# Late expert slots of an attention + two-layer-mixture kernel: rectifier in two halves over separate PSUM banks, weight scale step at the start of the split, last store inside the last branch

## The chip, the core and the metric

The kernel runs on one core of a Trainium2 chip. The core has a matrix engine (TensorE, PE in the profile, with its weight loads as PEld), three engines for elementwise work (VectorE = DVE, ScalarE = ACT, GpSimd = POOL), SyncE (SP), which issues most DMAs here, and 16 DMA engines. Each engine has its own instruction queue, worked off in order; queues wait for each other through semaphores. Matmul results land in PSUM (8 banks of 128 x 512 f32), everything else lives in SBUF.

The metric is the device time of one execution in microseconds, as the median of several executions: 1108.17 us for the kernel before (3 runs, 1105.92 to 1108.96).

## The reference, cut to what matters

```python
x = attention(q, k, v)          # queries pooled in pairs: 4 x 576 rows of 8 heads x 64 -> x is 2304 x 512
x = rational(x @ w_in) @ w_out  # w_in 512 x 2048, w_out 2048 x 512
logits = x @ w_gate             # 2304 x 8
e_idx = np.argmax(logits, axis=1)
for e in range(8):              # every token goes to one expert
    mask = e_idx == e
    h = np.maximum(x[mask] @ w1[e], 0.0)                                  # 512 x 1024
    out[mask] = gate_w[mask, None] * eom[mask, e, None] * (h @ w2[e])     # 1024 x 512
```

Only the last loop, the experts, is touched. How many tokens each expert has is known only while the kernel runs.

## The kernel before, in words

**Precision.** Every f32 operand of a matmul is kept as two f16 parts, high and low, and a product is three matmuls: high x high, high x low, low x high. A scale (a power of two) brings each operand into the range of f16; it comes from the largest absolute value.

**Stages.** Attention, the rational layer and the sorting of tokens by expert are recorded by a planner, which sets the order of every engine by a table and by costs; that part, with the first five blocks of experts' work, is not touched: its instructions stand in the same order before and after. The tokens, sorted by expert, lie in DRAM (`ysort`) and are worked off in slots of 128 tokens of one expert. Slots 0 to 4 (`NEARLY = 5`) are planned beside the last of the rational layer. Slots 5 and up, the late slots, are plain code: the functions `slot`, `from_slot`, `weights` and `changed` write instructions in the order in which they are called, and each engine works off its share in that order.

**A slot.** `slot_prep` loads 128 rows, finds their scale, splits them into high and low f16 and transposes them by DMA (`xTq`). `slot_g1` is the first product: 8 groups `fc` of 12 matmuls (L1476 to L1478), each group into 128 columns of one PSUM tile of 1024 columns (`sab0` or `sab1`, two banks each); then ACT writes the high part of the rectified result (L1483), DVE the low part (L1484), and DVE a scale (L1485). `slot_g2` is the second product: one DVE scale (L1504), 8 x 3 matmuls of 512 columns (L1494 to L1496) into `shared` or `hbs[0]`, ACT's scaled copy to SBUF (L1506), and POOL's indirect DMA to the tokens' places in the output (L1500, "the store").

**Order in the late slots.** `slot(s)` runs g1(s) and, around it, g2(s-1): from slot 6 to slot 16 the second product of the slot before stands behind the first product of this one, so PE has work while ACT and DVE rectify. In slot 17 (`NFULL - 1`) it also stands behind; from slot 18 (`NFULL`) on it stands ahead of g1(s), and the last slot's g2 comes alone at the end (`from_slot`, in the `Else`). Slot 18 and later ones sit in nested `If`s on the number of slots in use, which a register holds.

**Changing experts.** `changed(s, engines, fn)` reads a flag from SBUF into a register on each of those engines and branches: if slot s begins a new expert, its weights are split. `wsplit` gives the steps for one of the two weight matrices: DVE's largest value (4096 columns, L478), POOL's reduction over partitions (L1443), DVE's scale from it (`scale2`, L1422 to L1424), then four times ACT's high part (L500) and DVE's low part (L511) of 1024 columns, then DVE's copy of the inverse scale (L1450). `weights(s, xs, parts)` takes the steps in two parts: part 0 two slots ahead (the `SIZE` engines, DVE and POOL), part 1 one slot ahead or in the slot (the `SPLIT` engines, DVE and ACT). Of the 19 slots that this input uses, slot 18 alone begins a new expert among the late ones.

**The check.** Behind slot 9 `checks()` tests on the fly that the fixed scales fitted; it has one tiny matmul (L1008) into the bank `yps`.

**The end.** After the last store all engines read a number (L1801) and branch (L1802) on whether the first expert had too few tokens for the planned slots; that is not so here, and the branch jumps over the spare path, which holds a second, general copy of the whole kernel. Then the program's closing barrier (L1864).

Of the kernel before, what the change touches and what calls it, by code (L numbers as in the profile page):

```python
# [12 lines left out]
I32 = mybir.dt.int32  # L13
AF = mybir.ActivationFunctionType
# [329 lines left out]
def whole(tc, general, keep, checked, q, k, v, w_in, w_out, moe_a, moe_b, w_gate, w_ogate, w1, w2, out):  # L344
    nc = tc.nc
    V, S, G, T, SP = Steps(nc.vector), nc.scalar, nc.gpsimd, nc.tensor, nc.sync
    B, H, L, D = q.shape
    NT, DM = out.shape
# [8 lines left out]
    MUL, ADD, SUB, MAX = ALU.mult, ALU.add, ALU.subtract, ALU.max  # L357
# [4 lines left out]
    NEARLY = 5  # L362
# [15 lines left out]
    sab = [keep("psum", [128, 1024], F32, name=f"sab{i}") for i in range(2)]  # L378
    shared = keep("psum", [128, 512], F32, name="shared")
    sc_ = shared[:, 384:512]  # L380
    pvb = shared[:, 0:4 * (D + 1)].rearrange("p (n d) -> p n d", n=4)
    hbs = [keep("psum", [128, 512], F32, name=f"hps{i}") for i in range(2)]
    yps = keep("psum", [128, 512], F32, name="yps")
# [4 lines left out]
    def tiny(n, dt=F32):  # L388

        o = used[0]  # L390
        used[0] += n
        assert used[0] <= 944
        return small[:, o:o + n] if dt is F32 else small[:, o:o + n].bitcast(dt)
# [955 lines left out]
    FE = F // 128  # L1349
# [19 lines left out]
    rws = [zcut(RW, F32) for _ in range(5)]  # L1369
# [4 lines left out]
    obs = [zcut(DM, F32) for _ in range(2)]  # L1374
# [5 lines left out]
    xsm = [tiny(6) for _ in range(8)]  # L1380
    fst = tiny(4 * NE)
    fsti = tiny(4, I32)
    firstm = tiny(NE)
    padrows = keep("dram", [128, RW], F32, name="padrows")

# [48 lines left out]
    def wsplit(s, x, early=False):  # L1434

        fr = (raws1, raws2)[x][s % 3]
        m, M, sc, inv = (t[:, 2 * (s % 3) + x:2 * (s % 3) + x + 1] for t in (wm, wM, wq, wpn))
        fh, fl = ((w1h, w1l), (w2h, w2l))[x]
        steps = [({"DVE": 4.4}, amax(m, fr, AX.X))]
        if early:  # L1440
            steps += [m, lambda M: lambda e: scale2(M, m.bitcast(I32), sc, inv, 8)]
        else:
            steps += [({"POOL": 0.4}, lambda e: G.partition_all_reduce(M, m, channels=128,  # L1443
                                                                       reduce_op=bass_isa.ReduceOp.max)),
                      ({"DVE": 0.7}, lambda e: scale2(M, m.bitcast(I32), sc, inv))]
        for c in range(0, 4096, 1024):
            cs = slice(c, c + 1024)
            steps.append(({"ACT": 0.99, "DVE": 0.62}, hi(fh[:, cs], fr[:, cs], lambda: sc)))
            steps.append(({"DVE": 1.15, "POOL": 3.4}, lo(fl[:, cs], fr[:, cs], fh[:, cs], lambda: sc)))
        steps.append(({"DVE": 0.07}, lambda e: V.tensor_copy(wps[:, x:x + 1], inv)))  # L1450
        return steps
# [15 lines left out]
    def slot_g1(s):  # L1467
        t, xT = xsm[s % 8], xTq[s % 2][0].rearrange("p (k t) -> p k t", k=2 * KD)
        hp = sab[s % 2]

        def mm(fc):
            def f(e):
                o = hp[:, fc * 128:(fc + 1) * 128]
                for kc in range(KD):
                    a, b = w1hk[:, kc, fc * 128:(fc + 1) * 128], w1lk[:, kc, fc * 128:(fc + 1) * 128]
                    T.matmul(o, a, xT[:, kc], start=(kc == 0), stop=False)  # L1476
                    T.matmul(o, a, xT[:, KD + kc], start=False, stop=False)  # L1477
                    T.matmul(o, b, xT[:, kc], start=False, stop=(kc == KD - 1))  # L1478
            return ({"PE": 0.67}, f)

        hh, hl = hhs[s % 2][0], hls[s % 2][0]
        return [mm(fc) for fc in range(FE)] + [
            ({"ACT": 1.0}, lambda e: S.activation(hh, hp, AF.Relu)),  # L1483
            ({"DVE": 1.2}, lambda e: V.scalar_tensor_tensor(out=hl, in0=hp, scalar=0.0, in1=hh, op0=MAX, op1=SUB)),  # L1484
            ({"DVE": 0.19}, lambda e: V.tensor_scalar(t[:, 4:5], rws[s % 5][0][:, DM:DM + 1], t[:, 3:4], wps[:, 0:1],  # L1485
                                                      op0=MUL, op1=MUL))]

    def slot_g2(s):
        t, o, ob = xsm[s % 8], shared if s < NEARLY or s % 2 else hbs[0], obs[s % 2][0]

        def mm(fc):
            def f(e):
                a, b = hhs[s % 2][0][:, fc * 128:(fc + 1) * 128], hls[s % 2][0][:, fc * 128:(fc + 1) * 128]
                T.matmul(o, a, w2hk[:, fc], start=(fc == 0), stop=False)  # L1494
                T.matmul(o, a, w2lk[:, fc], start=False, stop=False)
                T.matmul(o, b, w2hk[:, fc], start=False, stop=(fc == FE - 1))  # L1496
            return ({"PE": 0.64}, f)

        def put(e):
            G.indirect_dma_start(  # L1500
                out=out, out_offset=bass.IndirectOffsetOnAxis(ap=rws[s % 5][0][:, DM + 1:DM + 2].bitcast(I32), axis=0),
                in_=ob, in_offset=None, bounds_check=NT - 1, oob_is_err=False)

        return [({"DVE": 0.19}, lambda e: V.tensor_scalar(t[:, 5:6], t[:, 4:5], wps[:, 1:2], None, op0=MUL))] + \  # L1504
            [mm(fc) for fc in range(FE)] + [
            ({"ACT": 0.6}, lambda e: S.activation(ob, o, AF.Copy, scale=t[:, 5:6])), ({"POOL": 1.05}, put)]  # L1506

    def first_slots(key):

# [206 lines left out]
    def do(steps):  # L1716
        for engines, fn in steps:
            fn(list(engines)[0])
# [21 lines left out]
    def weights(s, xs=(0, 1), parts=(0, 1)):  # L1740

        for p in parts:
            for x in xs:
                do(wsplit(s, x)[3 * p:None if p else 3])

    def one_by_one():
        for s in range(NEARLY):
            if s > 0:
                changed(s, [ET.SP], lambda: load_w(s))
                changed(s, WE, lambda: weights(s))  # L1750
            else:
                load_w(s)
                weights(s)
            load_rows(s)
            do(slot_prep(s))
            do(slot_g1(s))
            do(slot_g2(s))
# [21 lines left out]

    def from_slot(s):  # L1780
        if s == NSL:
            do(slot_g2(s - 1)[1:])
            return
        with tc.If(used_slots[0] > s) as there:  # L1784
            slot(s)
            from_slot(s + 1)
        with there.Else():
            do(slot_g2(s - 1)[1:])

    for s in range(NEARLY, NEARLY + 3):  # L1790
        changed(s, [ET.SP], lambda: load_w(s))
# [2 lines left out]
    for s in range(NEARLY, NFULL):  # L1794
# [3 lines left out]
        if s == NEARLY + 4 and not general:  # L1798
            checks()
    from_slot(NFULL)  # L1800
    full = nc.values_load(fsti[0:1, 3:4], engines=ALLE, min_val=0, max_val=NT)  # L1801
    with tc.If(full < 128 * NEARLY):  # L1802
        if general:
            one_by_one()
        else:
            fits = nc.values_load(fsti[0:1, 2:3], engines=ALLE, min_val=0, max_val=1)
            with tc.If(fits < 1) as unfit:
                checked()
            with unfit.Else():
                one_by_one()  # L1810

# [55 lines left out]
```

## Time and profile before

| | |
|---|---|
| median of 3 runs | 1108.17 us |
| the profiled execution | 1104.09 us |
| its span in the trace | 1102.2 us |
| PE busy | 923.3 us, 84% of the span |
| DVE busy | 868.2 us, 79% |
| ACT busy | 726.6 us, 66% |
| POOL busy | 566.3 us, 51% |
| first products of all slots (L1476 to L1478), PE | 3 x 106 us |

The profiled execution is 1.9 us longer than its span and 4.1 us under the median. Busy shares are means over stages that have different limits: up to about 880 us all engines are busy side by side, and from there on, in the late slots, PE works while the others have slack. What a step of the late slots is worth is therefore read from the idle times of PE there and from what ended them. Times within the trace are counted from the start of the span.

### The profile page before, as it was taken

The page shows a single profiled execution, that of the slowest core. Times are in us where ns is not written, and L with a number is a line of the kernel's source. Part 1 is how long each engine was busy: PE and PEld are TensorE (multiplying, and loading weights), DVE is VectorE, ACT ScalarE, POOL GpSimd, SP SyncE. Part 2 cuts the span into 40 slices and gives each one's busy share as a digit, 9 for nine tenths or more (in the row PEclk, how much of TensorE's full clock was granted, in tenths as well). Part 3 has the DMA queues.
Part 4 walks back from the last instruction along what each step waited for, and adds up shares of the span by engine and source line. Part 5 has one row for each costly group of instructions (what it writes and reads, how often), then busy time and mean ns, then how long its engine had stood idle before and what let it go on. Part 6 is the DMA issues. An engine that isn't in the chain of part 4 may idle for free. (4 is left out here: it accounts for less than half of the span.)

```text
span 1102.2 us, 30178 instructions
## 1 busy us (share of the span) xinstructions
PE 923.3 (84%) x12138; PEld 660.7 (60%) x12138; DVE 868.2 (79%) x1727; ACT 726.6 (66%) x1132; POOL 566.3 (51%) x396
## 2 busy tenths in 40 slices
PE   0144678877789999999998889999999998999984
PEld 0022555655557766777776657677777675776742
DVE  6998888888888999998998998998898843333452
ACT  2364578777779888898887888899877511222222
POOL 1034267785568766667776567686845611010110
PEclk9955699999899999999999999999999999999997
DMA  8899999999999999899999999999864324333530
GB/s 300 269 252 286 222 194 190 195 212 210 203 191 172 208 186 203 170 158 179 158 193 178 188 171 187 218 152 163 145 111 147 76 59 98 78 73 74 174 87 17
DMA packets 493493, 185.91 MB, mean 169 GB/s; under 512 B 454596, under 2 KB 473028, under 8 KB 493253
## 3 DMA queue, kind: packets, MB, share of 16 engines
q1 hardware_dynamic: 490365, 174.26, 81.5%
q0 software_dynamic: 2960, 9.46, 2.5%
q8 instruction: 99, 1.62, 0.6%
q14 instruction: 69, 0.57, 0.2%
HBM read 60.45 MB, written 11.82 MB: 66 GB/s over the span
## 5 line engine op out<-in xcount | busy, mean ns | idle before, releaser
L1148 PE MATMUL hps<-scr,winh 128*128 128x128 f16 x1152 | 210.1, 222 | 9.1 <-DVE scr L1159 7.0
L1149 PE MATMUL hps<-scr,winh 128*128 128x128 f16 x1152 | 210.0, 222 | 0.0
L1150 PE MATMUL hps<-scr,winl 128*128 128x128 f16 x1152 | 209.9, 222 | 0.0
L761 POOL TENSOR_TENSOR att<-att 128x1152 f16<-128x1152 f32 x69 | 169.3, 2453 | 52.3 <-ACT att L755 27.6
L718 PE MATMUL sab<-att 128*128 128x512 f16 x512 | 138.9, 397 | 54.0 <-DMA att<-att 46.5
L728 DVE TENSOR_REDUCE small<-sab 128x1 f32<-128x1024 f32 x144 | 175.1, 1217 | 10.9 <-PE sab L718 8.1
L770 PE MATMUL shared<-att 128*128 128x65 f16 (+3 forms) x4320 | 151.0, 198 | 38.9 <-DMA att<-att 21.5
L770 PEld LDWEIGHTS <-att 128*128 128x128 f16 (+1 forms) x4320 | 141.0, 103 | 65.0 <-DMA att<-att 32.0
L746 ACT ACTIVATE att<-sab,small 128x1024 f32<-128x1024 f32 x144 | 159.9, 1111 | 12.8 <-DVE small L740 9.5
L718 PEld LDWEIGHTS <-att 128*128 128x128 f16 x768 | 69.8, 101 | 143.8 <-issue 62.2
L1149 PEld LDWEIGHTS <-winh 128*128 128x128 f16 x1152 | 113.8, 99 | 27.7 <-issue 11.6
L1163 POOL TENSOR_TENSOR scr<-scr 128x512 f16<-128x512 f32 (+1 forms) x77 | 103.4, 1345 | 48.3 <-ACT scr L1207 18.2
L1148 PEld LDWEIGHTS <-winh 128*128 128x128 f16 x1152 | 114.5, 99 | 19.5 <-issue 2.2
L1150 PEld LDWEIGHTS <-winl 128*128 128x128 f16 x1152 | 113.8, 99 | 0.0
L1476 PE MATMUL sab<-att 128*128 128x128 f16 x608 | 106.0, 221 | 7.0 <-DMA att<-att 4.9
L1215 PE MATMUL yps<-wouth,scr 128*128 128x512 f16 x288 | 109.9, 381 | 2.0 <-DVE small L493 1.4
L1217 PE MATMUL yps<-wouth,scr 128*128 128x512 f16 x288 | 109.8, 381 | 1.7 <-POOL scr L1163 1.3
L1216 PE MATMUL yps<-woutl,scr 128*128 128x512 f16 x288 | 109.8, 381 | 0.0
L1478 PE MATMUL sab<-att 128*128 128x128 f16 x608 | 105.9, 221 | 2.4 <-DVEq L1732 1.8
L1477 PE MATMUL sab<-att 128*128 128x128 f16 x608 | 105.9, 221 | 0.0
L1500 POOL DMA_INDIRECT out_dram<-att x19 | 19.0, 997 | 164.3 <-ACTq L1732 116.3
L755 ACT CAST att<-att 128x1152 f16<-128x1152 f32 x66 | 76.1, 1153 | 20.3 <-DMA att<-att 19.5
(219 smaller groups left out, 2250.9 us busy)
## 6 DMA issues: line engine op xcount, KB each, us to landing
att<-in_k_dram SPq DMA_DIRECT2D x16, 576.0 KB, 5.0
att<-in_q_dram SPq DMA_DIRECT2D x16, 512.0 KB, 4.7
att<-in_moe_w_dram SPq DMA_DIRECT2D x4, 2048.0 KB, 8.9
att<-in_v_dram SPq DMA_DIRECT2D x14, 576.0 KB, 4.8
scr<-in_moe_w_out_dram SPq DMA_DIRECT2D x12, 512.0 KB, 4.7
att<-ysort SPq DMA_DIRECT2D x19, 257.0 KB, 2.7
scr<-in_moe_w_in_dram SPq DMA_DIRECT2D x8, 512.0 KB, 8.5
woutl<-in_moe_w_in_dram SPq DMA_DIRECT2D x6, 512.0 KB, 7.5
```

The source lines that it names most:

```text
L718: T.matmul(dst[:, d0:d0 + w], qT[:, H * x + 2 * i + t, :], rhs, start=(x == 0), stop=(x == 1))
L728: A(key - ahead - .6, {"DVE": 1.13}, lambda e: V.tensor_reduce(out=mm[:, 0, bi:bi + 1], in_=ab, axis=AX.X, op=MAX, negate=True), r=[f"sab{ ...
L746: return lambda e: S.activation(dst, src, AF.Exp, bias=mm[:, 2, bi:bi + 1], scale=escale)
L761: lambda e: eng(e).tensor_tensor(out=phs[pb][:, 1], in0=p32, in1=ph(), op=SUB),
L770: T.matmul(pvb[p0:p0 + w, bi, 0:d], pt[:, lhs, p0:p0 + w], rhs[:, h, c, :], start=(c == 0 and lhs == 0 and rhs is vh), stop=(lhs == 2 * KC ...
L1148: T.matmul(hp, wh, xh[:, kc, :], start=(kc == 0), stop=False)
L1149: T.matmul(hp, wh, xl[:, kc, :], start=False, stop=False)
L1150: T.matmul(hp, wl, xh[:, kc, :], start=False, stop=(kc == KD - 1))
L1215: T.matmul(yps, a, wouth[:, ff, :], start=(ff == 0), stop=False)
L1216: T.matmul(yps, a, woutl[:, ff, :], start=False, stop=False)
L1217: T.matmul(yps, b_, wouth[:, ff, :], start=False, stop=(ff == KF - 1))
L1476: T.matmul(o, a, xT[:, kc], start=(kc == 0), stop=False)
```

## The change

Three edits, all in the code of the late slots:

1. The rectifier of a late slot works on two halves of 512 columns instead of one tile of 1024: four groups of matmuls, ACT and DVE on them, four more groups, ACT and DVE again. The halves lie in different PSUM tiles: the first 512 columns of `sab0` and of `sab1` in even slots, the two `hbs` tiles in odd ones. The second product of even slots moves from `hbs[0]` to `yps`.
2. `weights` takes two steps as part 0 and the rest as part 1: `scale2` leaves the `SIZE` branch, where it stood behind POOL's reduction, and becomes the first step of the `SPLIT` branch.
3. The store of the last slot is no longer issued in the `Else` of `from_slot`. The last slot's result always goes to `obs[0]`, DVE copies its row numbers to `lasti`, and POOL issues the store inside the final `If` or its new `Else`, behind the branch.

```diff
     def slot_g1(s):
         hp = sab[s % 2]
+        halves = hbs if s % 2 else [a[:, 0:512] for a in sab]
...
-                o = hp[:, fc * 128:(fc + 1) * 128]
+                o = hp[:, fc * 128:(fc + 1) * 128] if s < NEARLY else halves[fc // 4][:, fc % 4 * 128:(fc % 4 + 1) * 128]
...
-        return [mm(fc) for fc in range(FE)] + [
-            ({"ACT": 1.0}, lambda e: S.activation(hh, hp, AF.Relu)),
-            ({"DVE": 1.2}, lambda e: V.scalar_tensor_tensor(out=hl, in0=hp, scalar=0.0, in1=hh, op0=MAX, op1=SUB)),
+        def relu(x, o, w):
+            return [({"ACT": 1.0}, lambda e: S.activation(hh[:, o:o + w], x, AF.Relu)),
+                    ({"DVE": 1.2}, lambda e: V.scalar_tensor_tensor(out=hl[:, o:o + w], in0=x, scalar=0.0, in1=hh[:, o:o + w],
+                                                                    op0=MAX, op1=SUB))]
+
+        mms_ = [mm(fc) for fc in range(FE)]
+        if s < NEARLY:
+            steps = mms_ + relu(hp, 0, 1024)
+        else:
+            steps = mms_[0:4] + relu(halves[0], 0, 512) + mms_[4:8] + relu(halves[1], 512, 512)
+        return steps + [
...
-        t, o, ob = xsm[s % 8], shared if s < NEARLY or s % 2 else hbs[0], obs[s % 2][0]
+        t, o, ob = xsm[s % 8], shared if s < NEARLY or s % 2 else yps, obs[0 if last else s % 2][0]
...
-            ({"ACT": 0.6}, lambda e: S.activation(ob, o, AF.Copy, scale=t[:, 5:6])), ({"POOL": 1.05}, put)]
+            ({"ACT": 0.6}, lambda e: S.activation(ob, o, AF.Copy, scale=t[:, 5:6])),
+            ({"DVE": 0.07}, lambda e: V.tensor_copy(lasti, row)) if last else ({"POOL": 1.05}, put)]
...
-                do(wsplit(s, x)[3 * p:None if p else 3])
+                do(wsplit(s, x)[2 * p:None if p else 2])
...
         with there.Else():
-            do(slot_g2(s - 1)[1:])
+            do(slot_g2(s - 1, True)[1:])
...
-    with tc.If(full < 128 * NEARLY):
+    with tc.If(full < 128 * NEARLY) as short:
+        do([({"POOL": 1.05}, put_last)])
...
+    with short.Else():
+        do([({"POOL": 1.05}, put_last)])
```

Where the change moves instructions, three places in the order of the engines. The first is DVE in slot 18, from the branch that splits the second weight matrix to the end of the rectifier (`att` is the SBUF zone of the expert stage, `small` holds the scales, `sab` and `hps` are PSUM). Before:

```order
L1731 TENSOR_LOAD att
L1731 ISA x2
L1732 COMPARE_AND_BRANCH
L511 SCALAR_TENSOR_TENSOR att<-att,small 128x1024 x4
L1450 COPY small<-small 128x1
L1732 UNCONDITIONAL_BRANCH x3
L1484 SCALAR_TENSOR_TENSOR att<-sab_75,att 128x1024
L1485 TENSOR_SCALAR small<-att,small 128x1
```

The same place in the changed kernel (its line numbers are higher by 1 to 16):

```order
L1747 TENSOR_LOAD att
L1747 ISA x2
L1748 COMPARE_AND_BRANCH
L1423 TENSOR_SCALAR small<-small 128x1
L1424 TENSOR_SCALAR small<-small 128x1
L1425 TENSOR_SCALAR small<-small 128x1
L511 SCALAR_TENSOR_TENSOR att<-att,small 128x1024 x4
L1451 COPY small<-small 128x1
L1748 UNCONDITIONAL_BRANCH x3
L1486 SCALAR_TENSOR_TENSOR att<-hps_77,att 128x512
L1486 SCALAR_TENSOR_TENSOR att<-hps_78,att 128x512
L1495 TENSOR_SCALAR small<-att,small 128x1
```

The three instructions of `scale2` now stand inside the branch, ahead of the low parts, and the rectifier's low part is two instructions. (The piece is the first of several written copies of this code; the one for slot 18 reads `sab` instead of `hps`.)

The second place is PE around the check's matmul, behind the second product of slot 8. Before:

```order
L1495 MATMUL hps_77<-att 128x512
L1496 LDWEIGHTS att
L1496 MATMUL hps_77<-att 128x512
L1732 UNCONDITIONAL_BRANCH x2
L1008 LDWEIGHTS ones_82
L1008 MATMUL yps<-small,ones_82 128x1 [waits DVE_49]
```

And in the changed kernel:

```order
L1509 MATMUL yps<-att 128x512
L1510 LDWEIGHTS att
L1510 MATMUL yps<-att 128x512
L1748 UNCONDITIONAL_BRANCH x2
L1008 LDWEIGHTS ones_82 [waits DVE_49]
L1008 MATMUL yps<-small,ones_82 128x1 [waits Activation_49]
```

The check's matmul now writes the bank that the product just before it filled, and waits for ACT.

The third place is POOL at the end of the late slots. Before, in one of the `Else`s and behind it (the `ISA` rows raise the counters of stores that were not issued):

```order
L1500 DMA out_dram<-att 2304x512
L1784 ISA
L1784 UNCONDITIONAL_BRANCH
L1801 TENSOR_LOAD small
L1802 COMPARE_AND_BRANCH
```

And in the changed kernel, where the same store row stands a second time at the end of the program, in the `Else`, with one such `ISA` row (L1818) and then the closing barrier behind it:

```order
L1800 ISA
L1800 UNCONDITIONAL_BRANCH
L1817 TENSOR_LOAD small
L1818 COMPARE_AND_BRANCH
L1499 DMA out_dram<-att,small 2304x512
```

The register load and the branch stand ahead of the last store now.

## Rows read from the trace of the kernel before

**Rows 1.** Stretches: length, busy per engine (PE, PEld, DVE, ACT, POOL), PEclk, DMA, GB/s.

```profile
980.00:1000.00 20.00, 20.00 (x225) 14.33 (x223) 6.47 (x17) 4.87 (x6) 1.94 (x2) 1.00 0.36 69
...
1056.00:1058.00 2.00, 2.00 (x22) 2.00 (x21) 2.00 (x1) 0.00 (x0) 0.00 (x0) 0.50 0.00 0
...
1084.00:1086.00 2.00, 2.00 (x6) 0.63 (x5) 0.22 (x1) 0.00 (x0) 0.00 (x0) 0.50 0.02 4
```

**Rows 2.** Waits of PE from 860 us on: us in total, times, longest us.

```profile
PE sab L1476 <- DMA att<-att: 4.9, 2, 3.2
```

**Rows 3.** Instructions in order of time, slots 5 to 6: start, us, what [idle before].

```profile
931.40 1.02 ACT L1483 ACTIVATE att<-sab 128x1024 f16<-128x1024 f32 x1 [4.69 <-PE sab L1478]
...
932.46 1.22 DVE L1484 SCALAR_TENSOR_TENSOR att<-sab,att 128x1024 f16<-128x1024 f32 x1 [4.96 <-ACTq L1732]
...
933.98 0.23 PE L1478 MATMUL sab<-att 128*128 128x128 f16 x1 [1.17 <-DVEq L1732]
```

**Rows 4.** The same view: ACT and DVE on 512 columns from PSUM.

```profile
861.99 0.56 ACT L1189 COPY scr<-hps 128x512 f32<-128x512 f32 x1
...
864.54 0.68 DVE L1159 SCALAR_TENSOR_TENSOR scr<-scr,hps 128x512 f32<-128x512 f32 x1
```

**Rows 5.** The same view, at the check behind slot 9.

```profile
976.28 0.69 ACT L1506 ACTIVATE att<-hps,small 128x512 f32<-128x512 f32 x1 [4.15 <-PE hps L1496]
...
976.60 0.16 PE L1008 MATMUL yps<-small,ones 128*128 128x1 bf16 x1 [0.40 <-DVE small L1007]
```

**Rows 6.** The same view, slots 16 and 17.

```profile
1043.61 4.42 DVE L478 TENSOR_REDUCE small<-att 128x1 f32<-128x4096 f32 x1 [0.43 <-DMA att<-in_moe_w_dram]
1052.56 0.15 DVE L1422 TENSOR_SCALAR small<-small 128x1 int32<-128x1 int32 x1 [4.53 <-POOL small L1443]
...
1053.13 1.23 DVE L1484 SCALAR_TENSOR_TENSOR att<-sab,att 128x1024 f16<-128x1024 f32 x1
...
1053.75 0.22 PE L1476 MATMUL sab<-att 128*128 128x128 f16 x1 [3.18 <-DMA att<-att]
...
1054.65 0.23 PE L1478 MATMUL sab<-att 128*128 128x128 f16 x1 [0.63 <-DVEq L1732]
```

**Rows 7.** The same view, slot 18; in between one line's queue instructions, first and last start.

```profile
1068.54 4.27 ACT L500 ACTIVATE att<-att,small 128x1024 f16<-128x1024 f32 x4 [0.62 <-SPq L1732]
...
1069.72 4.87 DVE L511 SCALAR_TENSOR_TENSOR att<-att,small 128x1024 f16<-128x1024 f32 x4 [2.67 <-ACT att L500]
...
1075.78 4.25 ACT L500 ACTIVATE att<-att,small 128x1024 f16<-128x1024 f32 x4
...
L1732 DVEq COMPARE_BRANCH  x2: 50/53/56, 1076.1 to 1077.5; - x2
...
1077.74 4.87 DVE L511 SCALAR_TENSOR_TENSOR att<-att,small 128x1024 f16<-128x1024 f32 x4 [2.72 <-ACT att L500]
...
1082.59 1.22 DVE L1484 SCALAR_TENSOR_TENSOR att<-sab,att 128x1024 f16<-128x1024 f32 x1
...
1083.86 0.61 PE L1496 MATMUL hps<-att 128*128 128x512 f16 x1 [1.31 <-DVE att L1484]
```

**Rows 8.** The end: last copy and store, then single lines' queue instructions (durations ns, starts).

```profile
1091.46 0.69 ACT L1506 ACTIVATE att<-hps,small 128x512 f32<-128x512 f32 x1 [10.52 <-PEq L1802]
...
1092.43 0.97 POOL L1500 DMA_INDIRECT out_dram<-att  x1 [15.30 <-POOLq L1784]
...
L1802 POOLq COMPARE_BRANCH  x1: 50/50/50, 1094.3 to 1094.3; - x1
...
L1802 POOLq EVENT_SEMAPHORE  x6: 17/30/43, 1096.8 to 1097.3; - x6
...
L1802 POOLq INC_SWDGE_SEM  x1: 896/896/896, 1097.4 to 1097.4; - x1
...
L1864 POOLq DRAIN  x3: 46/107/3097, 1098.3 to 1101.9; - x3
...
DMA to landing us min/median/max: 2.6/2.6/2.6
```

More of the change, by code (lines that the diff above doesn't have):

```diff
@@ L1382, in whole @@
     fsti = tiny(4, I32)
+    lasti = tiny(1, I32)
     firstm = tiny(NE)
@@ L1481, in slot_g1, with put_last, slot_g2 @@
         hh, hl = hhs[s % 2][0], hls[s % 2][0]
-        return [mm(fc) for fc in range(FE)] + [
-            ({"ACT": 1.0}, lambda e: S.activation(hh, hp, AF.Relu)),
-            ({"DVE": 1.2}, lambda e: V.scalar_tensor_tensor(out=hl, in0=hp, scalar=0.0, in1=hh, op0=MAX, op1=SUB)),
+        def relu(x, o, w):
[8 more added lines that the diff above has]
+        return steps + [
             ({"DVE": 0.19}, lambda e: V.tensor_scalar(t[:, 4:5], rws[s % 5][0][:, DM:DM + 1], t[:, 3:4], wps[:, 0:1],
                                                       op0=MUL, op1=MUL))]
-    def slot_g2(s):
-        t, o, ob = xsm[s % 8], shared if s < NEARLY or s % 2 else hbs[0], obs[s % 2][0]
+    def put_last(e):
+        G.indirect_dma_start(out=out, out_offset=bass.IndirectOffsetOnAxis(ap=lasti, axis=0),
+                             in_=obs[0][0], in_offset=None, bounds_check=NT - 1, oob_is_err=False)
+    def slot_g2(s, last=False):
+        t, o, ob = xsm[s % 8], shared if s < NEARLY or s % 2 else yps, obs[0 if last else s % 2][0]
         def mm(fc):
@@ L1502, in put @@
                 in_=ob, in_offset=None, bounds_check=NT - 1, oob_is_err=False)
+        row = rws[s % 5][0][:, DM + 1:DM + 2].bitcast(I32)
         return [({"DVE": 0.19}, lambda e: V.tensor_scalar(t[:, 5:6], t[:, 4:5], wps[:, 1:2], None, op0=MUL))] + \
             [mm(fc) for fc in range(FE)] + [
-            ({"ACT": 0.6}, lambda e: S.activation(ob, o, AF.Copy, scale=t[:, 5:6])), ({"POOL": 1.05}, put)]
+            ({"ACT": 0.6}, lambda e: S.activation(ob, o, AF.Copy, scale=t[:, 5:6])),
+            ({"DVE": 0.07}, lambda e: V.tensor_copy(lasti, row)) if last else ({"POOL": 1.05}, put)]
     def first_slots(key):
@@ L1787, in from_slot @@
         with there.Else():
-            do(slot_g2(s - 1)[1:])
+            do(slot_g2(s - 1, True)[1:])
     for s in range(NEARLY, NEARLY + 3):
```

## The prediction

> **What bounds the kernel now.** I read the stretches first. In the middle of the late slots PE is busy for all of 20.00 us of 20 at full clock, with DVE at 6.5 and ACT at 4.9 [rows 1]: there a shorter rectifier is worth nothing, for the second product of the slot before covers it. So I went on to PE's waits in the late slots. The longest in sum is for a DMA [rows 2], the transposed rows of slot 17, 3.18 us, queued behind weight loads [rows 6]; the change leaves it alone. What is left are places without such a cover: from slot 5 to 6, the check, slots 16 to 17 and slot 18, where new weights are split, and the end. I read each in order of time, and take the terms from there. Minus is a gain.
>
> **Slot 5 to 6: -0.95 us.** No second product stands between the two first products. PE ends slot 5's at about 931.4, ACT starts there, DVE starts at 932.46 and ends 1.22 later, at 933.68, and PE's third matmul of slot 6 starts at 933.98, 0.30 later [rows 3]. With halves only the second one is left when PE ends. The trace has no rectifier of 512 columns. Below, half of the wide ones is 0.51 on ACT and 0.61 on DVE [rows 3]; nearest are a copy of 512 columns from PSUM on ACT, 0.56, and DVE's same operation, 0.68 [rows 4]; above stands ACT's scaled copy, 0.69 [rows 5]. I take 0.60 and 0.68: 931.40 + 0.60 + 0.04 + 0.68 + 0.30 = 933.02, a gain of 0.96 (0.9 to 1.1 with the ends). From there on PE is the bound again up to the check, so it stays.
>
> **The check: +0.4 us.** Its matmul writes `yps`, which slot 8's second product now fills, so it waits until ACT has copied that out. Before, ACT's copy starts at 976.28 and takes 0.69, up to 976.97; PE's matmul starts at 976.60, held by DVE [rows 5]. DVE will be early now, by the shorter rectifier, but ACT cannot be: 976.97 + 0.05 - 976.60 = 0.42. Queued behind it on PE is the whole first product of slot 10. With the DVE wait alone it would be 0, so the bounds are 0 and 0.5.
>
> **Slots 16 to 17: -0.65 us.** DVE ends the largest value of w1 at 1048.03, waits for POOL's reduction until 1052.56, and only then does the scale and, at 1053.13, slot 16's rectifier; PE has its transposed rows at 1053.75 but is held again until 1054.65, with 0.63 of idle, by DVE [rows 6]. Without the scale DVE is through by about 1050. The 0.63 goes; what is late then is the transfer, at 1053.75 as before. The 4.5 us that DVE wins are worth no more than that. PE still falls to half clock behind this gap (0.50 from 1056 to 1058) [rows 1]; the gap shrinks from 3.8 to 3.2 us, which may or may not spare that. Bounds -0.6 and, if it does, -1.6 (2 us at half clock hold work for 1).
>
> **The scale in slot 18: +1.75 us.** For w1 the scale is free in its new place: DVE waits for ACT there anyway, 2.67 us [rows 7]. For w2 it is not. Before, ACT starts the high parts at 1075.78, since the scale was made two slots earlier; DVE gets through its branches at 1077.5 and starts the low parts at 1077.74 [rows 7]. Now ACT has to wait until DVE has passed those branches and done the scale: 1077.6 + 0.57 (three instructions, 1052.56 to 1053.13 [rows 6]) + 0.1 = 1078.3. The low parts follow the high ones by 1.18 (1068.54 to 1069.72 [rows 7]): 1079.5 in place of 1077.74. Everything behind it on DVE, the low parts (4.87) and slot 18's rectifier, is on the path to the last product. Bounds: 0 if DVE came through early enough, 2.0 with a slower hand-over.
>
> **Slot 18's rectifier: -0.55 us.** DVE's 1.22 stands between the end of the low parts and PE's restart at 1083.86 [rows 7]. The last product can start on the first half: 0.68 instead of 1.22. The second half comes 0.7 later, under the first half of the product. PE idles 1.2 us longer ahead of this product than before (1.75 - 0.55) and ran it at half clock already (0.50 at 1084) [rows 1]; I cost the longer gap at nothing, 0.7 either way.
>
> **The end: -4.0 us.** After the store's issue at 1092.43 POOL does, in order, a counter raise, a register load, the branch at 1094.3, a first instruction behind the branch at 1096.8, one more raise at 1097.4 (0.90), and a drain of 3.10 from 1098.3 [rows 8], then 0.8 us of closing barrier. Load and branch now stand ahead of the store, in the 15.3 us that POOL idles for ACT [rows 8], and so does the new copy of the row numbers on DVE. Behind the store are left the raise, the drain and the barrier. The raise starts 4.97 after the store's issue before (1092.43 to 1097.4); it will start between 0.2 and 1.5 after it, and I take 1.0. The data land 2.6 after the issue [rows 8], inside the drain if that does not wait for them. Bounds -4.7 and, if the drain starts only with the landing, -3.3.
>
> Here the row speaks against a rule. The row shows 2.5 us from the branch at 1094.3 to POOL's next instruction [rows 8]. The Trainium skill, Advanced Engine Details and Errata, section Control Flow Timing, has about 108 ns for a compare-and-branch. By that figure moving the branch saves 2.4 us less, and the whole sum would be -1.6. The sum goes by the row.
>
> **Sum.** -0.95 + 0.4 - 0.65 + 1.75 - 0.55 - 4.0 = -4.0. The profiled execution took 1104.09 us (span 1102.2 and 1.9 around it), so it would take 1100.1. It is 4.1 under the median of the runs, 1108.17; the terms are waits and instructions that do not depend on that, so the median goes to 1104.2. The many late slots in the middle give nothing, and half of what the tail wins is given back by the scale of w2.
>
> **The rivals.**
>
> *The end pays the branch all the same.* The last store lies in an `Else` far from the code before it, and POOL still has to leave it. If leaving it costs a gap like the 2.5 us behind the branch [rows 8], or those 2.5 us are not the branch's and come again, the end gains 1.5, the sum is -1.5, and the time 1106.7. For it: the same engine, the same kind of jump. (A cheap branch, as in that page's figure, would mean the second of the two.) Against: the closing drain starts right behind the last raise already (1097.4 + 0.90 = 1098.3 [rows 8]), and nothing is added between the two. Chance 0.22.
>
> *The tail gives more.* The scale of w2 costs nothing, because DVE comes through its branches before ACT is free: -5.75, 1102.4. Or the shorter gap before slot 17 spares the half clock: -1.0 or more on top of -4.0, 1103.2 or less. For the first: DVE gains time in slots 16 and 17. Against it: its branches end at 1077.5, 1.7 us behind ACT's start [rows 7], the change takes none of them away, and DVE comes to them from the low parts of w1, which follow ACT. For the second: the gap is 0.6 shorter. Against it: 3.2 us of idle remain. Chance 0.20.
>
> *Slower: reading PSUM while PE writes.* ACT and DVE now read the first half while PE fills the second, in 14 late slots. If that held PE's matmuls up by more than 0.52 us a slot, about 5% of a slot (120 of the 225 matmuls in 20 us [rows 1], 10.7 us), the 7.3 us lost would turn -4.0 into +3.3; at 0.7 us a slot the time is 1108.17 - 4.0 + 9.8 = 1114. Against it: the rectifier of a slot already reads its banks while PE writes others, and PE is at 20.00 of 20 all the same [rows 1]. The Trainium skill, PSUM — Partial Sum Buffer, section Summary: rules for kernel authors, says to aim at a different bank for reading while a matmul runs, which is what the halves do; no row shows the two on one bank. Chance 0.05.
>
> **How the numbers follow.** My forecast has 0.53, with its own range from 1102.7 to 1105.7. From no change the chip's runs can be told at about 0.3%, 3.3 us, so faster means under 1104.85: 0.38 of the forecast's 0.53, 0.18 of the larger gain's 0.20, 0.01 of the first rival, together 0.57. The first rival and the rest of the forecast give 0.37 within 0.3%. Slower has 0.06. The range runs from 1100.3, the larger gain with some scatter, to 1108.4, where the first rival's scatter ends.
>
> **What would show it.** In the new trace: PE's wait at the start of slot 6 down from 2.6 to about 1.6 us in all; the check's matmul held by ACT for 0.8 after slot 8's product; no wait for DVE in slot 17 behind the one for the transfer; DVE's `scale2` right before the low parts of w2, and ACT's high parts starting after it instead of 1.9 us ahead of the low ones; PE's last product starting some 0.7 us behind one half of a rectifier; and from the last store's issue to the end 5.7 us instead of 9.8. The forecast is wrong if the end still holds a gap of 2 us or more between store and barrier, if the middle slots' period of 10.7 us moves at all, or if slot 18 is as fast as before in spite of the scale.

## The result: more gain than was forecast

The changed kernel took 1099.12 us in the median of its runs, the kernel before 1109.09 in the median of eight: ratio 0.9909, 95% interval 0.9885 to 0.9932, so 7.5 to 12.8 us less. One of its eight executions took 1257.21 us at a mean granted clock of 0.743; the ratio is that of the seven others, which took 1096.33 to 1101.84. The forecast was 4.0 less, 1104.2, with a range that ended at 1100.3. A second comparison (below) gave 0.9945 (0.9925 to 0.9964), 4 to 8 us less. The two intervals meet at about 0.993, 7.5 to 8 us.

The profiled execution took 1096.37 us, with a span of 1094.0 (before 1104.09 and 1102.2). Not all of those 8.2 us are the change's. The part that the planner orders, which the diff leaves alone, ended 1.25 us earlier in this execution: its last product ends at 923.63 instead of 924.88. In all the profiles of this study that end lies between 923.26 and 929.31. So executions are compared here by the **distance** from the end of that product to the end of the span: 177.33 us before, 170.37 after, 6.96 less. (One expectation below has distances of 170.9 and 169.1, from rounded spans; here they are 170.8 and 169.0.)

PE's waits in the late slots of the changed kernel, in order of time (start, length, instruction, idle before it and what ended it). L1478 to L1480 are first products, L1508 to L1510 second ones, L1008 the check:

```profile
923.25 0.38 PE L1510 MATMUL shared<-att 128*128 128x512 f16 x1
924.57 0.23 PE L1478 MATMUL hps<-att 128*128 128x128 f16 x1 [0.94 <-ACTq L1748]
...
930.84 0.23 PE L1478 MATMUL sab<-att 128*128 128x128 f16 x1 [0.73 <-ACTq L1748]
...
932.11 0.23 PE L1480 MATMUL sab<-att 128*128 128x128 f16 x1 [0.99 <-DVEq L1748]
...
975.16 0.16 PE L1008 MATMUL yps<-small,ones 128*128 128x1 bf16 x1 [0.82 <-ACTq L1748]
...
1051.94 0.22 PE L1478 MATMUL hps<-att 128*128 128x128 f16 x1 [2.81 <-DMA att<-att]
...
1057.29 0.38 PE L1508 MATMUL yps<-att 128*128 128x512 f16 x1
1057.51 0.38 PE L1509 MATMUL yps<-att 128*128 128x512 f16 x1
...
1078.38 0.61 PE L1508 MATMUL yps<-att 128*128 128x512 f16 x1 [3.29 <-ACT att L1485]
...
1080.36 0.61 PE L1510 MATMUL yps<-att 128*128 128x512 f16 x1 [0.94 <-DVE att L1486]
```

Against [rows 3, 5 to 7]: the wait into slot 6 is shorter, the check's longer, the second wait in slot 17 (0.63, for DVE) is gone, and slot 17's first product lasts from 1051.94 to 1057.29, 5.35 us, where before it took from 1053.75 to 1061.54, that wait included. The stretches (length, busy per engine, PEclk, DMA) show why:

```profile
980.00:1000.00 20.00, 20.00 (x224) 14.34 (x222) 6.64 (x18) 5.21 (x8) 1.95 (x2) 1.00 0.37 80
1055.00:1057.00 2.00, 2.00 (x39) 2.00 (x37) 1.27 (x5) 0.44 (x1) 1.34 (x2) 1.00 0.00 0
1080.00:1082.00 2.00, 1.64 (x4) 0.58 (x5) 1.08 (x3) 0.00 (x0) 0.00 (x0) 0.50 0.00 0
```

In slot 17 PE ran at 2.4 GHz (1.00), before at 1.2 [rows 1]: 39 products in 2 us in place of 22. The last product starts at 1.2 GHz in both. The middle is as it was, 20.00 of 20.

DVE and ACT where slot 16 turns to 17 and in slot 18:

```profile
1042.26 4.42 DVE L478 TENSOR_REDUCE small<-att 128x1 f32<-128x4096 f32 x1 [0.59 <-DMA att<-in_moe_w_dram]
1046.60 1.28 DVE L1486 SCALAR_TENSOR_TENSOR att<-sab,att 128x512 f16<-128x512 f32 x2
...
1050.34 4.42 DVE L478 TENSOR_REDUCE small<-att 128x1 f32<-128x4096 f32 x1 [2.28 <-DMA att<-in_moe_w_dram]
```

```profile
1072.97 0.15 DVE L1423 TENSOR_SCALAR small<-small 128x1 int32<-128x1 int32 x1 [2.42 <-POOLq L1800]
...
1074.77 4.87 DVE L511 SCALAR_TENSOR_TENSOR att<-att,small 128x1024 f16<-128x1024 f32 x4 [1.26 <-ACT att L500]
1079.56 0.15 DVE L1451 COPY small<-small 128x1 f32<-128x1 f32 x1
1079.62 1.28 DVE L1486 SCALAR_TENSOR_TENSOR att<-sab,att 128x512 f16<-128x512 f32 x2
...
1073.58 4.27 ACT L500 ACTIVATE att<-att,small 128x1024 f16<-128x1024 f32 x4 [2.17 <-DVE small L1425]
1077.76 1.06 ACT L1485 ACTIVATE att<-sab 128x512 f16<-128x512 f32 x2
```

Slot 16's rectifier follows w1's largest value at once, 1046.60, where it waited 4.5 us for POOL before [rows 6]. In slot 18 the scale (L1423) stands ahead of ACT's high parts, as forecast, and these wait 2.17 us for it.

The end, the last store and the queue instructions around it (durations in ns, then starts):

```profile
1088.60 0.97 POOL L1499 DMA_INDIRECT out_dram<-att,small  x1 [15.94 <-POOLq L1818]
```

```profile
L1818 POOLq COMPARE_BRANCH  x1: 45/45/45, 1074.4 to 1074.4; - x1
L1818 POOLq INC_SWDGE_SEM  x1: 914/914/914, 1088.8 to 1088.8; - x1
...
L1499 POOLq MOVE  x1: 29/29/29, 1077.1 to 1077.1; - x1
...
L1883 POOLq DRAIN  x3: 52/107/3399, 1089.8 to 1093.7; - x3
```

The branch lies 14 us ahead of the store. One raise (0.91), the drain (3.40) and the closing barrier are all that is left behind it: 5.40 us from the store's issue to the end of the span, 9.79 before [rows 8].

### The profile page after: what moved, and what is told of

Same layout as the page of the kernel before. It is cut to its first block, busy times and chain, and to the rows that moved or that the text cites. A ratio compares the mean times of both kernels' runs of the same rounds, so it can differ in the third digit from the quotient of the medians.

```text
span 1094.0 us, 30221 instructions
## 1 busy us (share of the span) xinstructions
PE 926.9 (85%) x12138; PEld 663.7 (61%) x12138; DVE 875.3 (80%) x1742; ACT 729.2 (67%) x1146; POOL 568.6 (52%) x396
## 5 line engine op out<-in xcount | busy, mean ns | idle before, releaser
L718 PE MATMUL sab<-att 128*128 128x512 f16 x512 | 141.8, 403 | 52.2 <-DMA att<-att 45.2
L761 POOL TENSOR_TENSOR scr<-att,scr 128x1152 f16<-128x1152 f32 x28 | 68.2, 2435 | 19.7 <-ACT scr L755 13.0
L746 ACT ACTIVATE att<-shared,small 128x128 f32<-128x128 f32 x144 | 52.7, 366 | 36.7 <-DVE small L740 17.4
L731 DVE TENSOR_SCALAR_CACHE_REDUCE small<-shared,small 128x128 bf16<-128x128 f32 x144 | 49.9, 346 | 24.4 <-PE shared L718 9.2
```

Source lines behind the costliest of these rows:

```text
L718: T.matmul(dst[:, d0:d0 + w], qT[:, H * x + 2 * i + t, :], rhs, start=(x == 0), stop=(x == 1))
L746: return lambda e: S.activation(dst, src, AF.Exp, bias=mm[:, 2, bi:bi + 1], scale=escale)
L761: lambda e: eng(e).tensor_tensor(out=phs[pb][:, 1], in0=p32, in1=ph(), op=SUB),
```

## The experiments

In theory A the gain is the sum of separate steps; its rivals are named in each expectation. "Slot 17" below is the time from the end of slot 15's second product to that of slot 16's, 16.57 us before and 13.50 after.

**The three parts, each alone on the kernel before.**

```
e1: put_last, If(full < ...) as short / short.Else() of the diff; rest as before
e2: slot_g1 with relu() and halves, yps in slot_g2; rest as before
e3: -  do(wsplit(s, x)[3 * p:None if p else 3])
    +  do(wsplit(s, x)[2 * p:None if p else 2])
```

The last store:

> Alone: the last store inside the last branch; rectifier and scale step as in the kernel before. Theory A (the changed kernel's gain is a sum of separate steps, the largest of them the end): from the issue of the last store to the end 5.4 us in place of 9.8, nothing else moves, so about 4.4 us less than the kernel before, ratio 0.996; the half-clock stretch in slot 17 (3.4 us at 1.2 GHz while its first product runs) stays, as does the 0.63 us for which PE waits for VectorE there. Rival B (the branch at the end is paid all the same, and the gain of the changed kernel lies in the slots): 1.5 us less, ratio 0.9986.

Measured: 0.9968 (0.9940 to 0.9995), distance 173.3, 4.1 less. The interval holds the ratios of both theories, so the trace decides: the end, now 5.1 us, gave 4.7, and slot 17 took 16.99, 0.4 more. The branch at the end was the price, and B falls.

The halves:

> Alone: the rectifier in two halves over separate PSUM banks; store and scale step as in the kernel before. Theory A (the half-clock stretch before slot 17's product goes with the scale step): slot 5 to 6 0.6 us less, the check's matmul 0.4 more, slot 18 0.85 less (0.55 the rectifier, 0.3 the last product): together 1.0 us less, ratio 0.999, and the stretch at 1.2 GHz in slot 17 is there as before. Rival B (the stretch goes because the halves bring PE to slot 17 in another way): another 2 us less, 3 in all, ratio 0.997, and slot 17's first product runs at 2.4 GHz.

Measured: 0.9968 (0.9941 to 0.9996), distance 176.1, 1.3 less. A's terms are there: PE's two waits into slot 6 fell from 1.16 and 1.17 to 0.73 and 0.63 (0.97 in all), and between slot 18's first product and the restart in the last one 3.68 us stand in place of 4.29. The last product itself took 6.2 us in place of 7.4, with 3.4 us at 1.2 GHz in place of 6.8. Slot 17 ran at 1.2 GHz, against B, and took 17.45. This execution had its planned part end at 929.31, the latest of all: its own time, 1107.24, says nothing of the change.

The scale step:

> Alone: the scale step behind the other work, for both weight matrices; rectifier and store as in the kernel before. Theory A (the 0.63 us for which PE waits for VectorE in slot 17 and the half-clock stretch behind it both go with this step): 0.6 and 2.0 us less in slot 17, 1.5 more in slot 18 where the scale of w2 now stands in the branch: 1.1 less, ratio 0.999, and slot 17's first product at 2.4 GHz. Rival B (the stretch has another cause): it stays, and the sum is 0.9 us more, ratio 1.001.

Measured: 0.9993 (0.9965 to 1.0021), distance 177.9, 0.5 more. B came closer: the half-clock stretch stayed. The wait for DVE in slot 17 went, but the transfer came 0.76 us later in this execution, and slot 17 took 16.27. From slot 18's first product to the restart in the last one were 5.51 us in place of 4.29: w2's scale cost 1.2 here. The last two lines below are the start of slot 16's second product, which matters further down:

```profile
1054.49 0.22 PE L1476 MATMUL sab<-att 128*128 128x128 f16 x1 [3.94 <-DMA att<-att]
...
1061.48 0.38 PE L1494 MATMUL hps<-att 128*128 128x512 f16 x1
1061.69 0.38 PE L1495 MATMUL hps<-att 128*128 128x512 f16 x1
```

The three changes of distance add up to -4.8 us, close to the forecast's -4.0; the whole change has -6.96. What is over comes about in slot 17 (+0.4, +0.9 and -0.3 alone, -3.07 together), so the parts do not simply add there. Elsewhere the whole gained 1.9 us less than the parts, 0.9 of it in the last product, where the halves alone had the shorter stretch at 1.2 GHz.

**w2's scale back where it was, w1's moved.**

```
- do(wsplit(s, x)[2 * p:None if p else 2])
+ do(wsplit(s, x)[(2 + x) * p:None if p else 2 + x])
```

> The changed kernel, with the scale step moved for w1 alone: that of w2 stands behind w2's all-reduce in the slot before, as in the kernel before. Theory A (in slot 18 of the changed kernel the scale of w2 is on the chain, 1.5 us): the ACT high parts of w2 start 1.5 us earlier after slot 18's first product, the last product and the end too; slot 17's rectifier loses nothing since the all-reduce of w2 comes behind the row work of slot 18. 1.5 us less than the changed kernel, 11 to 12 less than the kernel before where that one had 10, ratio 0.9895. Rival B (VectorE is held by the wait for the all-reduce in front of slot 17's rectifier, as it was in slot 16): PE waits 0.6 us there and a half-clock stretch returns, about 1 us more than the changed kernel, ratio 0.992.

Measured: 0.9912 (0.9884 to 0.9940), distance 169.0. The last product shows the term by itself:

```profile
1079.46 0.61 PE L1508 MATMUL yps<-att 128*128 128x512 f16 x1 [2.27 <-ACTq L1748]
...
1080.88 0.61 PE L1510 MATMUL yps<-att 128*128 128x512 f16 x1 [0.39 <-DVE att L1486]
```

From the end of slot 18's first product (1077.19) to this restart are 3.69 us, in the changed kernel 5.27 (1075.09 to 1080.36): w2's scale cost 1.6. No wait for DVE came back in slot 17, but a stretch at 1.2 GHz did, behind the same 2.87 us of waiting for the transfer, and took 1.4 of it back (14.94). Two more differences go with this version: the last product took 5.89 us in place of 7.11, with 3.4 us at 1.2 GHz in place of 6.8, and PE's second wait into slot 6 is 0.63 again, where the changed kernel has 0.99.

The stretch in slot 17:

```profile
1053.00:1055.00 2.00, 2.00 (x22) 2.00 (x20) 2.00 (x1) 0.00 (x0) 0.00 (x0) 0.50 0.00 0
```

The same kernel once more:

> The changed kernel with w2's scale back in the slot before, once more, beside the other version on one chip. Theory A (it gains 1.3 us on the changed kernel at the last product, and pays up to 1.7 where slot 17 meets a half-clock stretch): from the last product of the planned part to the end of the span 167.5 to 169.5 us, ratio 0.992 to 0.994. Rival B (its 0.9912 is its true size): 0.991.

Measured: 0.9910 (0.9882 to 0.9938), distance 168.9. The ratio is B's, the distance A's. Slot 17 ran again at 1.2 GHz, behind 2.68 us of waiting, and took 14.71.

**The changed kernel once more**, unedited:

> The changed kernel once more, beside the kernel before on one chip. The parts alone gave 0.9968, 0.9968 and 0.9993, whose product is 0.993 (8 us), where the changed kernel had 0.991 with an interval of 0.9885 to 0.9932, and behind the end of the planned part its profile is 7.0 us shorter than that of before. Theory A (the change is worth 5 to 7 us behind the planned part, of which up to 2 hang on whether slot 17's first product meets a half-clock stretch; the rest of the 10 us was scatter of the planned part, whose last product ended between 923.6 and 929.3 us in the six profiles so far): ratio 0.993 to 0.9955, the stretch in slot 17 at 1.2 GHz may be there this time. Rival B (the change makes the planned part itself faster, or the stretch is gone for good): ratio 0.991 again, the last planned product ends before 924.5 us and slot 17 runs at 2.4 GHz.

Measured: 0.9945 (0.9925 to 0.9964), distance 170.8, 6.5 less than before. The planned part ended at 926.81 this time, 3.2 us later than in the first profile. In the changed kernel and the versions of it this end lies between 923.26 and 927.10, in the kernel before and those with one part alone between 923.82 and 929.31: no gain of the change is seen there, and the distances of the two executions differ by only 0.5. That the two ratios differ because of this part is likely and not shown, for each is the ratio of many runs and only one of them has a profile. Slot 17 took 13.60, at 2.4 GHz behind 2.90 us of waiting. So 2.4 GHz came twice out of two here, and not once out of two with w2's scale moved back, behind waits just as long: what decides it there stays open.

**PE's gaps filled with products that nobody reads**, in the version with w2's scale back and in the kernel before (there the first loop alone):

```
+ if s == NFULL - 2:
+     for _ in range(11):
+         T.matmul(yps, hhs[(s - 1) % 2][0][:, 0:128], w2hk[:, 0], start=True, stop=True)
+ if s == NFULL:
+     for _ in range(10):
+         T.matmul(hbs[0], w1hk[:, 0, 0:128], xTq[s % 2][0][:, 0:512], start=True, stop=True)
```

> The changed kernel with w2's scale back in the slot before, and with added products that nobody reads: 11 of 512 columns (2.4 us) into PE's wait ahead of slot 17, and 10 (2.2 us) into the one ahead of the last product. Theory A (the stretches at 1.2 GHz in slot 17 and in the last product come from PE's idle gaps just ahead of them): both run at 2.4 GHz; 3.4 us at half clock cost 1.7 in slot 17 where the stretch would have come, 1.7 to 3.4 in the last product: 2 to 4 us less than without the added products, ratio about 0.988. Rival B (the granted clock falls there for another reason): stretches of 3.4 or 6.8 us at 1.2 GHz remain, the time is unchanged or up to 0.5 us more where the added products run past the end of a wait, ratio 0.991.

Measured: 0.9948 (0.9930 to 0.9966), distance 173.6. In slot 17 A holds: 2.4 GHz, 13.95 us. At the last product it fails: PE waited there for something that the profile does not name, 1.39 and 2.54 us long, though ACT and DVE were through with the rectifier by 1080.9, and ran at 1.2 GHz all the same. The filler is no remedy.

```profile
1081.97 0.39 PE L1508 MATMUL yps<-att 128*128 128x512 f16 x1 [1.39 <-issue]
...
1084.91 0.61 PE L1509 MATMUL yps<-att 128*128 128x512 f16 x1 [2.54 <-issue]
```

A likely cause is in the DMA record, which also lists transfers of the kind `instruction`, the program's own code (queue, kind: packets, MB, share; 1082 to 1084 us):

```profile
q8 instruction: 1, 0.02, 3.1%
```

Such 16 KB transfers ran from 1079.39 to 1080.58 and from 1082.58 to 1083.58, and PE went on 1.39 and 1.33 us behind their ends. The same holds for two unnamed waits at this place with no product added there: in the next run (transfer to 1082.12, PE at 1083.61) and in the second execution with w2's scale back (1076.73, 1078.17). Queue 8 has 99 such transfers in the kernel before and 100 in both kernels with a filler, whose extra matmuls only PE runs. So PE most likely waited for its code; no run tests it.

> The kernel before with one addition: 11 products of 512 columns that nobody reads (2.4 us) in PE's wait ahead of slot 17's first product. Theory A (in slot 17 the stretch at 1.2 GHz follows the length of the idle time ahead of it: it was there in all four profiles with 3.8 us or more in all, in one of three with 2.8 to 2.9, in none of two with less than 1): with some 1.5 us of waiting left, slot 17's first product runs at 2.4 GHz, and from the last product of slot 15 to that of slot 16 it takes about 15 us where the kernel before took 16.6. Rival B (the fall has another cause): the 3.4 us at 1.2 GHz are there and the distance stays at 16 to 17 us.

Measured: one execution, 1103.31 us, distance 176.4; slot 17 at 2.4 GHz as A says, and yet 16.94 us, 0.4 more than without the filler. This run explains the most, though it is a single one. A new wait stands in the second product of slot 16, and DVE's queue ends it:

```profile
1055.50:1057.50 2.00, 2.00 (x40) 2.00 (x38) 1.41 (x1) 0.00 (x0) 0.00 (x0) 1.00 0.00 0
```

```profile
1061.06 0.15 DVE L1422 TENSOR_SCALAR small<-small 128x1 int32<-128x1 int32 x1 [0.56 <-POOL small L1443]
...
1062.63 0.21 DVE L1504 TENSOR_SCALAR small<-small 128x1 f32<-128x1 f32 x1 [1.04 <-DVEq L1732]
...
1062.59 0.38 PE L1495 MATMUL hps<-att 128*128 128x512 f16 x1 [1.73 <-DVEq L1732]
```

The second matmul of that product waits until DVE is past its next branch. DVE reaches that branch only when w2's largest value and scale for slot 18 are made; the branch itself is the one for slot 16's own second weights and is not entered. In the kernel before PE met the same release with a wait of only 0.27 us, which the profile does not mark: the stretch at half clock had made PE that late.

```profile
1061.54 0.38 PE L1494 MATMUL hps<-att 128*128 128x512 f16 x1
1062.02 0.38 PE L1495 MATMUL hps<-att 128*128 128x512 f16 x1
```

```profile
L1731 DVEq TENSOR_LOAD <-att x1: 310/310/310, 1061.1 to 1061.1; - x1
...
L1732 DVEq EVENT_SEMAPHORE  x1: 21/21/21, 1061.9 to 1061.9; - x1
```

The second of these fences is DVE's branch: its flag is read at 1061.1, just behind the scale, and it is left at 1061.9; the two matmuls start 0.48 us apart. With the scale step alone moved (e3) they start 0.21 apart and in the changed kernel 0.22 (1057.29, 1057.51, above), where DVE leaves its branch 2.7 us before it is needed:

```profile
L1748 DVEq EVENT_SEMAPHORE  x1: 21/21/21, 1054.8 to 1054.8; - x1
```

So two chains ended almost together in slot 17 of the kernel before: PE at half clock, and DVE with its two waits for POOL. Counted from the end of slot 15's second product, DVE's release came at 11.45 us before and at 11.81 with the filler, and that is the 0.4 that slot 17 took longer. Filling the gap takes PE's chain away and is worth nothing; moving the scale alone takes DVE's away and gave 0.3, with a transfer 0.76 later; in the changed kernel both were gone, 3.07 us.

**A better order.** The transfer that PE waits for in slot 17 is issued behind two loads of weights, 2 MB each. Two versions take w2's load from ahead of it, for slot 18 alone:

```
e7: load_w(18) loads w1 only; w2's load moves behind slot_prep(17),
    w2's maximum and scale behind w1's split in slot 17
e8: as e7, and in slot 17 one branch for both:
+ def both(s):
+     a, b = wsplit(s, 0), wsplit(s, 1)
+     do(a[2:3] + b[:2] + a[3:] + b[2:3])
```

> The changed kernel with w2's scale back before the branch, and for slot 18 alone the load of w2 issued behind the transposed rows of slot 17 (in place of ahead of them), its maximum taken behind the rectifier of slot 17. Theory A (PE's wait of 2.8 to 3.2 us ahead of slot 17 is the transposition standing in the queue behind 4 MB of weights): the wait falls to less than 0.5 us, the 0.9 us wait ahead of slot 17's second product and the 0.7 us in slot 18 go with it since VectorE comes to the rectifier earlier; 3 to 4.4 us less, ratio 0.988. Rival B (the transposition itself or the row work is the late one): the wait stays above 2 us, and w2 coming later makes the last product wait: 0 to 3 us more, ratio 0.991 to 0.994.

Measured: 0.9938 (0.9920 to 0.9957), distance 172.2. With w2's load gone from ahead of the transfer, slot 17 has no wait left and takes 10.54 us, at 2.4 GHz: the order in the queue was the cause. But the 0.9 us ahead of the next product and the 0.7 in slot 18 stayed, and B's cost came too: w2's maximum was last on DVE, and the last product waited.

```profile
1069.74 4.41 DVE L478 TENSOR_REDUCE small<-att 128x1 f32<-128x4096 f32 x1
...
1082.05 0.61 PE L1508 MATMUL yps<-att 128*128 128x512 f16 x1 [7.31 <-ACT att L1485]
```

> As the version with w2 loaded behind the transposed rows, but in slot 17 one branch does, in this order, w1's scale, w2's maximum, w1's split and w2's scale; before, w2's maximum stood behind w1's split on VectorE and ended at 1074.2 us, and the last product waited 7.3 us. Theory A (that wait was w2's maximum standing last on VectorE, which sat idle for 4.8 us ahead of w1's low parts): the maximum fits into that idle time, the last product starts about 3.5 us earlier, slot 17 keeps no wait of PE; from the last product of the planned part to the end of the span 166 to 167 us (177.3 in the kernel before, 170.4 and 170.9 in the changed kernel, 169.1 with w2's scale moved back), ratio 0.990. Rival B (w1's split is late instead, since its branch now holds the maximum): PE waits 2 to 4 us ahead of slot 18's first product and the distance stays at 169 to 171, ratio 0.993 to 0.9945.

Measured: 0.9908 (0.9875 to 0.9941), distance 167.0, the shortest of all, and 10.3 us under the kernel before. The maximum fits ahead of the low parts, and the last product waits 2.61 for ACT and then 1.85 for DVE:

```profile
1060.59 4.42 DVE L478 TENSOR_REDUCE small<-att 128x1 f32<-128x4096 f32 x1
1065.40 4.87 DVE L511 SCALAR_TENSOR_TENSOR att<-att,small 128x1024 f16<-128x1024 f32 x4 [0.39 <-ACT att L500]
...
1077.86 0.39 PE L1508 MATMUL yps<-att 128*128 128x512 f16 x1 [2.61 <-ACT att L1485]
```

By its median, 1095.67 us, it can't be told from the version with w2's scale back (1095.44 on the same chip); by the distance it is 1.9 us shorter, in one profile of each. That both beat the kernel before by some 0.9% is shown; that they beat the changed kernel rests on the distances, 1.3 to 1.9 and 3.4 to 3.8 us.

All profiles beside each other (us; waits are PE's, ahead of and in slot 17's two products):

| kernel | waits in slot 17 | clock of its first product | slot 17 | distance |
|---|---|---|---|---|
| before | 3.18 + 0.63 | 1.2 GHz | 16.57 | 177.3 |
| e1 store alone | 2.51 + 1.72 | 1.2 | 16.99 | 173.3 |
| e2 halves alone | 2.47 + 2.12 | 1.2 | 17.45 | 176.1 |
| e3 scale alone | 3.94 | 1.2 | 16.27 | 177.9 |
| e9 before, gap filled | 0.87 + 0.93 + 1.73 | 2.4 | 16.94 | 176.4 |
| changed | 2.81 | 2.4 | 13.50 | 170.4 |
| e5 changed again | 2.90 | 2.4 | 13.60 | 170.8 |
| e4, e10 w2's scale back | 2.87, 2.68 | 1.2 | 14.94, 14.71 | 169.0, 168.9 |
| e6 the same, gaps filled | 0.87 | 2.4 | 13.95 | 173.6 |
| e7 w2 behind the rows | none | 2.4 | 10.54 | 172.2 |
| e8 one branch | none | 2.4 | 10.54 | 167.0 |

## Why the prediction was wrong, step by step

Slots 16 to 17, forecast -0.65: this is **the step that failed**. The prediction put it so: "The 4.5 us that DVE wins are worth no more than that", that is, than the wait of 0.63 seen in the trace. Slot 17 gave 3.07: 0.63 of wait for DVE, 0.37 of a shorter wait for the transfer (which scatters: 2.47 to 3.94 us in the other executions without a filler or a moved load), 1.81 in the first product, where the half-clock stretch did not come, and 0.27 at the start of the second. What the prediction left out is that DVE's release held slot 16's second product too, at 1062, with hardly a wait to be seen. As long as that release stands, PE can win nothing ahead of it: a filled gap in the kernel before lost the stretch and gained nothing. The moved scale let DVE pass its branch 2.7 us before PE needs it.

The rival "the tail gives more" had the stretch, at "-1.0 or more", and came closest, but not the reason why losing it could be banked. Its 1.0, like the outer bound of -1.6, was priced from a row of 2 us; the stretch lasted 3.4 (1054.9 to 1058.3). That the clock did not fall is luck as far as these runs tell: the stretch came in all four executions with 3.81 to 4.59 us of waiting, and in two of the four with 2.68 to 2.90. In the two that had it (w2's scale back) slot 17 still gave 1.6 and 1.9. None of the prediction's own signs of being wrong came: the step that failed was one that they did not watch.

The end, forecast -4.0: -4.39, and -3.90 in the second execution, whose drain took 3.88 us in place of 3.40; both are inside its bounds. The raise came 0.2 us behind the store's issue, not 1.0. From the branch at 1074.4 to POOL's next instruction at 1077.1 are 2.7 us again, now in POOL's idle time, so the sum was right to go by the row. POOL's branch instruction itself took 50 ns before and 45 after; what was saved is above all the time from it to the next instruction. The Trainium skill's about 108 ns (Advanced Engine Details and Errata, Control Flow Timing) are the figure of a compare-and-branch: more than the instruction took here, and far less than the time behind it. The rival by which the branch is paid all the same is refuted by the last store alone.

The scale of w2, forecast +1.75: +1.6, shown by moving it back (+1.2 with the scale step alone). Slot 18's rectifier, forecast -0.55: -0.61, shown by the halves alone. Together they left +0.98 in the changed kernel (1.2 forecast), and the last product ran 0.33 faster, which was priced at nothing.

Slot 5 to 6, forecast -0.95: -0.97 with the halves alone, but -0.61 in both profiles of the changed kernel, where PE's second wait there is 0.99 in place of 0.63. That wait is for DVE's queue, which goes through a branch there, and not for the rectifier. It is 0.63 or 0.64 in all five versions with w2's scale back, so it came with moving that scale; why is open. The check, forecast +0.4: +0.42 (0.40 to 0.82).

Reading one PSUM bank while PE writes another cost nothing: from the check to the end of slot 15 the kernel before and the changed one both take 73.97 us. That agrees with the Trainium skill, PSUM — Partial Sum Buffer, Summary: rules for kernel authors, as far as separate banks go; no run put the two on one bank.

The sum of what was measured is -0.61 + 0.42 - 3.07 + 0.03 + 0.98 - 0.33 - 4.39 = -6.97, against 6.96 between the two distances (0.03 is what the small waits from there to slot 18's first product changed). With the slot 17 of the forecast it would be -4.5. The rest of the first 10 us is not explained by the trace: the planned part, 1.25 us earlier in this profile, varies by more than that between executions, and the second comparison gave 6 us.

## What to carry to other kernels

Where an engine arrives at a release just as it comes, hardly a wait is shown, and the release still binds: before pricing a faster chain, look up on every engine when the next release for the waiting one comes, not only the wait that the trace names. Where two chains end together, taking one away can be worth next to nothing (0.4 lost and 0.3 won here) and taking both more than their waits, so single parts need not add up. For a change of a few microseconds, compare executions from a landmark behind the part that scatters.

## What had not been expected of the hardware

Between two executions of unchanged instructions the planned part differed by up to 6 us (923.26 to 929.31). The granted clock in slot 17 was 2.4 GHz behind waits of 2.81 and 2.90 us and 1.2 GHz behind 2.68 and 2.87. PE's waits that no signal explains (1.39 and 2.54 us behind added products, 3.46 and 2.61 without) each ended 1.3 to 1.5 us behind the end of a 16 KB transfer of code. What ends a wait for DVE's queue can be a branch that DVE passes without entering it (flag read at 1061.1, left at 1061.9) and no computation.
